# Row products, softmax inside PV and a V-moving last head in a one-token attention block

## The chip, the cores and the metric

One core of one Trainium2 chip. The metric is the device time of one execution in microseconds (us); one execution is also profiled. A ratio below is the mean time of one kernel's runs over that of the other's of the same rounds, with a 95% interval; so it is not quite the ratio of the medians quoted beside it. The verdict calls two kernels the same when they lie within 2%.

The engines in the profile are PE (matmuls), PEld (its weight loads), DVE (vector), ACT (activation), POOL, and SP, whose queue issues the loads here. PSUM is where matmuls put their results. PV is the product of the softmax's weights with V; a *turn* is a small f32 matmul that makes columns of rows; the *cadence* is the time from one head to the next.

## The reference, cut to what matters

One token of an adaLN-conditioned block: a modulation vector, a layer norm, attention with 32 query heads over 8 key/value heads and 32768 cached positions, the output projection, and a small feed-forward part.

```python
mod = (silu(c) @ w_mod).reshape(1, 6, 1, 512)          # w_mod 3 MB
h = layernorm(x) * (1 + ca) + sa
q = h @ wq                                             # wq 4 MB; 32 heads of 128
scores = einsum('bhqd,bhkd->bhqk', q, k) * 128**-0.5   # K cache 64 MB
o = einsum('bhqk,bhkd->bhqd', softmax(scores), v)      # V cache 64 MB
x = x + ga * (o.reshape(1, 1, 4096) @ wo)              # wo 4 MB
h = layernorm(x) * (1 + cb) + sb
return x + gb * (relu(h @ w1) @ w2)                    # 1.75 MB each
```

For each byte of K and V there is very little arithmetic: every byte is loaded once and used for four query heads.

## The kernel before

All loads go through one queue into a ring of four slots, in a fixed order (`stream`). A load is issued when its slot is free, that is, when the matmuls or transposes that read the slot's old content are done. (Cuts are marked `# ...`.)

```python
ring = ctx.enter_context(tc.tile_pool(name="ring", bufs=4))
stream = [("wm",), ("wq",)] + [("k", 0, (2 * G, 2 * G + 1)) for G in range(NG)]
for g in range(LAST):
    for G in range(NG):
        stream += [(kind, gg, (2 * G, 2 * G + 1)) for kind, gg in (("k", g + 1), ("v", g))]
stream += [("v", LAST, (0, 1)), ("v", LAST, (2,)), ("wo", 0), ("wo", 1), ("v", LAST, (3,)), ("wo", 2)]
stream += [("w1",)] + [("w2", i) for i in range(len(W2P))]
```

Modulation and queries are column products: the weights are the stationary operand, and each matmul gives one column of 128 values.

```python
for hq in range(Hq):
    for kt in range(KT):
        nc.tensor.matmul(qT_ps[:, hq:hq + 1], lhsT=wq_sb[:, kt, hq * Dh:(hq + 1) * Dh],
                         rhs=hT[:, kt:kt + 1], start=(kt == 0), stop=(kt == KT - 1))
```

For each head, DVE transposes K, PE forms the scores (S), the softmax follows, and PV multiplies with V. Heads 0 to 6 move V through PE (16x512 outputs). The last head has V stationary (columns), because its result is then there at once.

```python
def softmax(g):
    # ... row maximum m_p
    nc.tensor.transpose(out=mT_ps[:], in_=m_p[:], identity=ident_f[:])
    # ... maximum of each query head: Mrow, Mexp
    nc.tensor.matmul(Mb_ps[:], lhsT=Mexp[:], rhs=ident_f[0:1, 0:1], start=True, stop=True)
    # ... exponentials on ACT, P_g transposed on DVE to PT_g, Lexp
    nc.tensor.matmul(L_ps[:], lhsT=ones_f[:], rhs=Lexp[:], start=True, stop=True)

for g in range(Hkv):
    # ... build_qbd(g + 1)
    for G in range(NG):
        for u in (2 * G, 2 * G + 1):
            if g + 1 < Hkv:
                scores(g + 1, u)
        for u in (2 * G, 2 * G + 1):
            if g == LAST and u == NTILE - 1:
                for i in range(len(WOP) - 1):
                    project(i)          # first two parts of wo, as columns
            pv(g, u)
    if g + 1 < Hkv:
        softmax(g + 1)                  # after PV of head g
    normalise(g)
    # ...
project(len(WOP) - 1)                   # last part of wo, then the feed-forward part
```

## Time and profile before

| | before |
|---|---|
| median of 4 runs (the three of the prediction and one more) | 357.52 us (357.09 to 357.79) |
| profiled span, mean PE clock | 355.8 us, 0.876 |
| instructions; PE busy; DVE busy | 4200; 274.2 us; 188.0 us |
| loads | 149.43 MB; DMA share 1.00 from 20 to 340 us |

PE's timeline after PV of one head, before (columns: start, length, engine, line, operation, in brackets the idle time before and what ended it):

```profile
92.96 0.38 PE L371 MATMUL Mb_ps<-ident_f,Mexp 1*128 1x1 f32 x2
93.70 1.05 PE L429 MATMUL oT_ps<-osel,X 16*128 16x4 f32 x8 [0.36 <-ACT nbias L373]
96.59 0.45 PE L386 MATMUL L_ps<-Lexp,ones_f 128*128 128x4 f32 x2 [1.84 <-DVE Lexp L384]
99.50 1.87 PE L343 MATMUL S_ps<-KTt,qbd 128*128 128x512 bf16 x4 [2.47 <-DVE KTt L334]
```

From 92.96 to 99.50 PE does 1.9 us of small work and no score or PV matmul. The groups of the page that add this up over all heads (line, engine, operation, tiles, count, then busy us and mean ns, then idle time just before and its main releaser):

```profile
L343 PE MATMUL S_ps<-KTt,qbd 128*128 128x512 bf16 x512 | 134.5, 423 | 29.8 <-DVE KTt L334 29.7
L334 DVE STREAM_TRANSPOSE KTt<-Ksb 128x2048 f32<-128x2048 f32 x64 | 142.6, 2279 | 21.1 <-DMA Ksb<-in_A_k_cache_dram 17.0
L386 PE MATMUL L_ps<-Lexp,ones_f 128*128 128x4 f32 x16 | 3.9, 314 | 13.0 <-DVE Lexp L384 13.0
L359 PE MATMUL mT_ps<-ident_f,m_p 128*1 128x128 f32 x8 | 2.2, 269 | 8.4 <-DVE m_p L357 8.4
```

PE waits 13.0 us for the softmax sum and 8.4 for the maximum.

### The profile page before, as it was taken

What the parts mean: (1) busy time and instruction counts of PE and PEld (TensorE: products, weight loads), DVE (VectorE), ACT (ScalarE), POOL (GpSimd) and SP (SyncE); (2) the same over time, 40 slices, a digit from 0 to 9 for tenths busy, and PEclk for the clock granted to TensorE, in tenths of its full rate; (3) what the DMA queues carried; (4) which work ended last, traced back from release to release, by engine and by line L of the source; (5) the groups of instructions that cost most, each with busy time, mean ns of one, the idle gap of its engine ahead of it and who ended that gap; (6) DMA issues with size and microseconds to landing.
All of it is one profiled execution on the core that took longest, in us unless ns stands there. A gap on an engine that the chain in (4) does not pass through costs nothing.

```text
span 355.8 us, 4200 instructions
## 1 busy us (share of the span) xinstructions
PE 274.2 (77%) x1859; PEld 129.9 (37%) x1859; DVE 188.0 (53%) x210; ACT 30.8 (9%) x74; POOL 8.5 (2%) x14
## 2 busy tenths in 40 slices
PE   0552875998689885998499849987799859987754
PEld 0540322343333342443244324433243324335753
DVE  8414696783297409661759157642937184832020
ACT  1022002201200120001100120012000110003000
POOL 9000000000000000000000000000000000000000
PEclk9999968799969996999699978998599969997555
DMA  8999999999999999999999999999999999999993
GB/s 321 442 422 440 431 427 442 429 425 438 435 426 438 431 422 446 427 431 440 424 442 435 422 443 427 431 437 427 431 437 428 427 438 433 424 437 424 408 411 130
DMA packets 6604, 149.69 MB, mean 421 GB/s; under 512 B 697, under 2 KB 698, under 8 KB 1594
## 3 DMA queue, kind: packets, MB, share of 16 engines
q1 hardware_dynamic: 6578, 149.43, 97.9%
q8 instruction: 14, 0.23, 0.2%
q14 instruction: 4, 0.03, 0.0%
q10 hardware_dynamic: 8, 0.00, 0.0%
HBM read 149.42 MB, written 0.00 MB: 420 GB/s over the span
## 4 chain that ended last, share of the span: by engine, by line
DMA 47%; PE 34%; DVE 14%; issue 3%; ACT 0%; SPq 0%; DVEq 0%
DMA Ksb<-in_A_k_cache_dram 42%; PE S_ps L343 18%; PE o_ps L412 12%; DVE KTt L334 11%; DMA Vsb<-in_A_v_cache_dram 3%; DMA w_sb<-in_B_w_dram 2%; PE oT_ps L402 1%; DVE PT_g L381 1%; PE oT_ps L429 1%; DVE S_g L349 1%; PE L_ps L386 0%; SPq L118 0%; PE attnT_ps L461 0%; PE mT_ps L359 0%; ACT X L426 0%
## 5 line engine op out<-in xcount | busy, mean ns | idle before, releaser
L343 PE MATMUL S_ps<-KTt,qbd 128*128 128x512 bf16 x512 | 134.5, 423 | 29.8 <-DVE KTt L334 29.7
L334 DVE STREAM_TRANSPOSE KTt<-Ksb 128x2048 f32<-128x2048 f32 x64 | 142.6, 2279 | 21.1 <-DMA Ksb<-in_A_k_cache_dram 17.0
L412 PE MATMUL o_ps<-Vsb,PT_g 128*16 128x512 bf16 x448 | 99.0, 379 | 0.0
L343 PEld LDWEIGHTS <-qbd 128*128 128x128 bf16 x512 | 53.8, 106 | 104.6 <-issue 53.8
L412 PEld LDWEIGHTS <-PT_g 128*16 128x16 bf16 x448 | 39.1, 90 | 56.8 <-issue 3.0
L436 DVE TENSOR_TENSOR oT_sb<-oT_ps,Linv 128x4 bf16<-128x4 f32 x8 | 1.3, 162 | 71.8 <-PE oT_ps L429 57.3
L349 DVE TENSOR_SCALAR_CACHE_REDUCE S_g<-S_ps 128x512 f32<-128x512 f32 x16 | 11.1, 691 | 41.3 <-PE S_ps L343 41.3
L314 ACT COPY qbd<-qrep_sb 32x128 bf16<-32x128 bf16 x32 | 9.4, 295 | 160.0 <-PE S_ps L343 158.9
L386 PE MATMUL L_ps<-Lexp,ones_f 128*128 128x4 f32 x16 | 3.9, 314 | 13.0 <-DVE Lexp L384 13.0
L426 ACT COPY X<-o_ps 16x512 f32<-16x512 f32 x7 | 4.0, 574 | 110.4 <-PE o_ps L412 110.4
L402 PE MATMUL oT_ps<-PT_g,Vsb 128*128 128x4 bf16 x256 | 7.3, 166 | 4.4 <-DMA Vsb<-in_A_v_cache_dram 2.8
L381 DVE STREAM_TRANSPOSE PT_g<-P_g 128x1024 bf16<-128x1024 bf16 x8 | 9.9, 1232 | 0.0
L429 PE MATMUL oT_ps<-osel,X 16*128 16x4 f32 x56 | 7.3, 250 | 2.5 <-ACT nbias L373 2.5
L197 PE MATMUL xc_ps<-one,c_bd 8*128 8x1 bf16 x4 | 0.3, 172 | 11.6 <-DVE c_bd L187 11.6
L376 ACT ACTIVATE P_g<-S_g,nbias 128x1024 bf16<-128x1024 f32 x8 | 9.2, 1147 | 0.2
L402 PEld LDWEIGHTS <-Vsb 128*128 128x128 bf16 x256 | 7.2, 105 | 4.5 <-DMA Vsb<-in_A_v_cache_dram 2.9
L359 PE MATMUL mT_ps<-ident_f,m_p 128*1 128x128 f32 x8 | 2.2, 269 | 8.4 <-DVE m_p L357 8.4
L386 PEld LDWEIGHTS L_ps<-Lexp,ones_f 128*128 128x128 f32 x16 | 3.6, 271 | 13.5 <-issue 13.4
L155 DVE COPY sel<-ident_bf 128x128 bf16<-128x128 bf16 x4 | 7.8, 3823 | 0.4 <-POOL ident_bf masks.py:199 0.4
L429 PEld LDWEIGHTS oT_ps<-osel,X 16*128 16x128 f32 x56 | 6.7, 186 | 3.1 <-ACT nbias L373 3.1
L292 PE MATMUL qT_ps<-hT,wq_sb 128*128 128x1 bf16 x128 | 3.6, 165 | 3.2 <-DMA wq_sb<-in_A_wq_dram 3.2
L359 PEld LDWEIGHTS mT_ps<-ident_f,m_p 128*1 128x1 f32 x8 | 0.6, 80 | 12.2 <-issue 9.2
(94 smaller groups left out, 79.4 us busy)
## 6 DMA issues: line engine op xcount, KB each, us to landing
Ksb<-in_A_k_cache_dram SPq DMA_DIRECT2D x16, 4096.0 KB, 29.7
Vsb<-in_A_v_cache_dram SPq DMA_DIRECT2D x15, 4096.0 KB, 25.5
wq_sb<-in_A_wq_dram SPq DMA_DIRECT2D x1, 4096.0 KB, 19.7
Vsb<-in_A_v_cache_dram SPq DMA_DIRECT2D x2, 2048.0 KB, 15.5
wm_sb<-in_w_mod_dram SPq DMA_DIRECT2D x1, 3072.0 KB, 10.2
wo_sb<-in_A_wo_dram SPq DMA_DIRECT2D x1, 2048.0 KB
wo_sb<-in_A_wo_dram SPq DMA_DIRECT2D x2, 1024.0 KB, 10.2
w_sb<-in_B_w_dram SPq DMA_DIRECT2D x1, 1792.0 KB, 10.5
```

The lines of the kernel that those rows point to most:

```text
L155: nc.vector.tensor_copy(out=sel[:, hp, :].rearrange("p (a c) -> p a c", a=4), in_=src)
L314: nc.scalar.copy(out=o, in_=i)
L334: nc.vector.transpose(out=KTt[:].bitcast(F32), in_=Ksb[:, 32 * half:32 * half + 32, :].rearrange("p j d -> p (j d)").bitcast(F32),)
L343: nc.tensor.matmul(S_ps[:], lhsT=qbd[g % 2][:, hp, s, :], rhs=KTv[:, 16 * sl:16 * sl + 16, h, :, par], start=(t4 == 0 and sl == 0 and hp = ...
L349: nc.vector.tensor_scalar(out=S_tiles[g][:, G, :], in0=S_ps[:], scalar1=1.0, scalar2=None, op0=ALU.mult, op1=ALU.max, accum_out=m_tiles[g] ...
L376: nc.scalar.activation(out=P_g[:], in_=S_g[:].rearrange("p g f -> p (g f)"), func=ACT.Exp, bias=nbias[:], scale=scale, accum_out=l_g[:],)
L381: nc.vector.transpose(out=PT_g[:], in_=P_g[:])
L386: nc.tensor.matmul(L_ps[:], lhsT=ones_f[:], rhs=Lexp[:], start=True, stop=True)
L402: nc.tensor.matmul(o_tiles[g][:], lhsT=Vsb[:, j, :], rhs=PT_g[:, c0:c0 + REP], start=(u == 0 and j == 0), stop=(u == NTILE - 1 and j == TK ...
L412: nc.tensor.matmul(o_tiles[g][:], lhsT=PT_g[:, c0:c0 + 16], rhs=Vsb.rearrange("p (s j) d -> p s j d", j=16)[:, :, j, :], start=(u == 0 and ...
L426: nc.scalar.copy(out=X[:], in_=oT_ps[:])
L429: nc.tensor.matmul(oT_ps[:], lhsT=X[:, s * Dh:(s + 1) * Dh], rhs=osel[:, s, :], start=(s == 0), stop=(s == 3),)
```

## The change

The intent: fewer and larger instructions on PE, and no hole in PE's work at the end of each head.

- Modulation, queries and the first two parts of wo become row products: the vector is the stationary operand (one column), the weights move, and four one-row outputs sit at partitions 0, 32, 64 and 96. Small f32 matmuls turn the rows into columns again.
- The softmax is a generator, and its steps are placed between chunks of PV of the head before. PE gets a fixed order: 8 PV, maximum transpose, 8 PV, maximum broadcast, 16 PV, sum.
- The last head's first half of PV moves V, as in the other heads; only its second half stays in columns.
- A third PSUM bank for scores, and one shared PSUM accumulator. The order of the loads is unchanged.

```diff
-    ps_s = ctx.enter_context(tc.tile_pool(name="ps_s", bufs=2, ...))
+    ps_s = ctx.enter_context(tc.tile_pool(name="ps_s", bufs=3, ...))
 # ... one of the two new helpers for rows:
+    def to_rows(dst, src_T, w, n):
+        for kt in range(KT):
+            for j in range(n):
+                nc.tensor.matmul(
+                    dst[j // 4][32 * (j % 4):32 * (j % 4) + 1, :], lhsT=src_T[:, kt:kt + 1],
+                    rhs=w[:, kt, j * 512:(j + 1) * 512], start=(kt == 0), stop=(kt == KT - 1), ...)
 # ... queries (modulation likewise):
+    to_rows(q_ps, hT, wq_sb, 8)
+    nc.scalar.copy(out=q_rows[:, 0, :], in_=q_ps[0])
+    nc.vector.tensor_copy(out=q_rows[:, 1, :], in_=q_ps[1])
+    for i in range(2):
+        for m in range(4):
+            nc.tensor.matmul(qT_ps[:, i, m, :], lhsT=q_rows[:, i, m * Dh:(m + 1) * Dh], rhs=rowsel[:], ...)
 # ... softmax(g) gets two yields: after Mexp and after Lexp
 # ... last head, V stationary only in its second half:
-        if g == LAST:
+        if g == LAST and u > 1:
 # ... order of the heads:
+            if g + 1 < Hkv and G == NG - 1:
+                stages = softmax(g + 1)
+                pv(g, 2 * G, range(8))
+                next(stages)
+                pv(g, 2 * G, range(8, 16))
+                next(stages)
+                pv(g, 2 * G + 1)
+                next(stages, None)
+                continue
 # ... last head, before its last V quarter: project(i) now as rows, then
+                    join_rows()
-        if g + 1 < Hkv:
-            softmax(g + 1)
```

More of the change, by code (lines that the diff above doesn't have):

```diff
@@ L76 @@
     spool = ctx.enter_context(tc.tile_pool(name="spool", bufs=2))
-    ps_s = ctx.enter_context(tc.tile_pool(name="ps_s", bufs=2, space=bass.MemoryType.PSUM))
+    ps_s = ctx.enter_context(tc.tile_pool(name="ps_s", bufs=3, space=bass.MemoryType.PSUM))
     ps_o = ctx.enter_context(tc.tile_pool(name="ps_o", bufs=2, space=bass.MemoryType.PSUM))
@@ L181 @@
     oA = [const.tile([P, n * REP, P // (n * REP)], BF16, name=f"oA{i}") for i, (_, n) in enumerate(WOP)]
+    rowsel = const.tile([P, 4], F32)
+    nc.vector.tensor_copy(out=rowsel[:], in_=ident_f[:].rearrange("p (j c) -> p j c", c=32)[:, :, 0])
+    rowsum = const.tile([P, 1], F32)
+    nc.vector.reduce_sum(out=rowsum[:], in_=rowsel[:], axis=AX.X)
     one8 = const.tile([8, 1], BF16)
@@ L200, with bank, row_bank @@
     cT, xT = xc[:, 0, :], xc[:, 1, :]
-    attnT_ps = ps_acc.tile([P, KT], F32)
-    nc.vector.memset(attnT_ps[:], 0.0)
+    acc_ps = ps_acc.tile([P, REP + KT], F32)
+    nc.vector.memset(acc_ps[:], 0.0)
+    oT_ps, attnT_ps = acc_ps[:, 0:REP], acc_ps[:, REP:REP + KT]
+    def bank(name):
+        return ps_s.tile([P, 512], F32, tag="s", name=name)[:]
+    def row_bank(name):
+        t = bank(name)
+        nc.vector.memset(t, 0.0)
+        return t
     def layernorm_T(src_T, stat_in, dst_T, shiftT, nscaleT, tagp):
@@ L243, with rows_sb @@
     nc.vector.tensor_tensor(out=siluT[:], in0=cT, in1=sig[:], op=ALU.mult)
-    modT_ps = small_ps([P, NMOD], "modT_ps")
-    for j in range(6):
-        for ko in range(KT):
-            for kt in range(KT):
-                lhsT = wm_sb[:, kt, j * D:(j + 1) * D].rearrange("p (m ko) -> p ko m", ko=KT)
-                nc.tensor.matmul(
-                    modT_ps[:, j * KT + ko:j * KT + ko + 1], lhsT=lhsT[:, ko, :], rhs=siluT[:, kt:kt + 1],
-                    start=(kt == 0), stop=(kt == KT - 1),
-                )
-    modT_sb = const.tile([P, NMOD], F32)
-    nc.vector.tensor_copy(out=modT_sb[:], in_=modT_ps[:])
+    def to_rows(dst, src_T, w, n):
[3 more added lines that the diff above has]
+                    dst[j // 4][32 * (j % 4):32 * (j % 4) + 1, :], lhsT=src_T[:, kt:kt + 1],
+                    rhs=w[:, kt, j * 512:(j + 1) * 512], start=(kt == 0), stop=(kt == KT - 1),
+                    skip_group_check=True,
+                )
+    mod_ps = [row_bank(f"mod_ps{i}") for i in range(2)]
+    to_rows(mod_ps, siluT, wm_sb, 6)
+    def rows_sb(name):
+        return spool.tile([P, 2, 512], F32, tag="S_g", name=name)
+    mod_rows = rows_sb("mod_rows")
+    nc.scalar.copy(out=mod_rows[:, 0, :], in_=mod_ps[0])
+    nc.vector.tensor_copy(out=mod_rows[:, 1, :], in_=mod_ps[1])
+    modT_ps = small_ps([P, 2, KT, 4], "modT_ps")
+    for i in range(2):
+        for ko in range(KT):
+            nc.tensor.matmul(
+                modT_ps[:, i, ko, :], lhsT=mod_rows[:, i, :].rearrange("q (m ko) -> q ko m", ko=KT)[:, ko, :],
+                rhs=rowsel[:], start=True, stop=True,
+            )
+    modT_sb = const.tile([P, 8 * KT], F32)
+    nc.vector.tensor_copy(
+        out=modT_sb[:].rearrange("p (i j ko) -> p i ko j", i=2, j=4), in_=modT_ps[:],
+    )
     def rows4(src_T, r_ps, name):
@@ L269, in rows4 @@
         return r_sb
-    gb_ps = ps_s.tile([P, 512], F32, tag="s", name="gb_ps")[:, 0:P]
+    gb_ps = bank("gb_ps")[:, 0:P]
     nc.vector.memset(gb_ps, 0.0)
@@ L288 @@
     wq_sb = need(("wq",))
-    qT_ps = small_ps([P, Hq], "qT_ps")
-    for hq in range(Hq):
-        for kt in range(KT):
+    q_ps = [row_bank(f"q_ps{i}") for i in range(2)]
+    to_rows(q_ps, hT, wq_sb, 8)
+    q_rows = rows_sb("q_rows")
+    nc.scalar.copy(out=q_rows[:, 0, :], in_=q_ps[0])
+    nc.vector.tensor_copy(out=q_rows[:, 1, :], in_=q_ps[1])
+    qT_ps = small_ps([P, 2, 4, 4], "qT_ps")
+    for i in range(2):
+        for m in range(4):
             nc.tensor.matmul(
-                qT_ps[:, hq:hq + 1], lhsT=wq_sb[:, kt, hq * Dh:(hq + 1) * Dh],
-                rhs=hT[:, kt:kt + 1], start=(kt == 0), stop=(kt == KT - 1),
+                qT_ps[:, i, m, :], lhsT=q_rows[:, i, m * Dh:(m + 1) * Dh], rhs=rowsel[:], start=True, stop=True,
             )
     qT_sb = const.tile([P, Hq], BF16)
-    nc.scalar.copy(out=qT_sb[:], in_=qT_ps[:])
+    nc.scalar.copy(out=qT_sb[:].rearrange("p (i j m) -> p i m j", i=2, j=4), in_=qT_ps[:])
     qrep_ps = small_ps([P, 4, Hq], "qrep_ps")
@@ L328, in scores @@
         if u % 2 == 0:
-            S_ps_tiles[g] = ps_s.tile([P, 512], F32, tag="s", name="S_ps")
+            S_ps_tiles[g] = bank("S_ps")
         S_ps = S_ps_tiles[g]
@@ L343, in scores @@
                     nc.tensor.matmul(
-                        S_ps[:], lhsT=qbd[g % 2][:, hp, s, :], rhs=KTv[:, 16 * sl:16 * sl + 16, h, :, par],
+                        S_ps, lhsT=qbd[g % 2][:, hp, s, :], rhs=KTv[:, 16 * sl:16 * sl + 16, h, :, par],
                         start=(t4 == 0 and sl == 0 and hp == 0), stop=(t4 == 3 and sl == 1 and hp == 3),
@@ L349, in scores, with pe_order @@
                 nc.vector.tensor_scalar(
-                    out=S_tiles[g][:, G, :], in0=S_ps[:], scalar1=1.0, scalar2=None,
+                    out=S_tiles[g][:, G, :], in0=S_ps, scalar1=1.0, scalar2=None,
                     op0=ALU.mult, op1=ALU.max, accum_out=m_tiles[g][:, G:G + 1],
                 )
+    def pe_order(instr):
+        tc.stamp_issue_order_token(instr.ins, "pe_pv")
     def softmax(g):
@@ L358, in softmax @@
         mT_ps = small_ps([1, P], "mT_ps")
-        nc.tensor.transpose(out=mT_ps[:], in_=m_p[:], identity=ident_f[:])
+        pe_order(nc.tensor.transpose(out=mT_ps[:], in_=m_p[:], identity=ident_f[:]))
         Mrow = spool.tile([1, 4], F32, tag="Mrow", name="Mrow")
@@ L369, in softmax @@
         )
+        yield
         Mb_ps = small_ps([P, 1], "Mb_ps")
-        nc.tensor.matmul(Mb_ps[:], lhsT=Mexp[:], rhs=ident_f[0:1, 0:1], start=True, stop=True)
+        pe_order(nc.tensor.matmul(Mb_ps[:], lhsT=Mexp[:], rhs=ident_f[0:1, 0:1], start=True, stop=True))
         nbias = spool.tile([P, 1], F32, tag="nbias", name="nbias")
@@ L384, in softmax @@
         nc.vector.tensor_scalar(out=Lexp[:], in0=mask4, scalar1=l_g[:], scalar2=None, op0=ALU.mult)
+        yield
         L_ps = small_ps([P, REP], "L_ps")
@@ L389, in softmax, with pv @@
         Linv_tiles[g] = Linv
-    def pv(g, u):
-        PT_g = PT_tiles[g]
+    def pv(g, u, js=range(16)):
+        PT_g = PT_tiles[g][:].rearrange("p (h j c) -> p h j c", h=2, c=32)[:, u // 2]
+        s0 = 4 * (u % 2)
         Vsb = need(("v", g, u))
-        G, s0 = u // 2, 4 * (u % 2)
-        if g == LAST:
-            if u == 0:
-                o_tiles[g] = ps_o.tile([P, REP], F32, tag="oT", name="oT_ps", bufs=1)
+        if g == LAST and u > 1:
             for j in range(TK):
-                c0 = (16 * G + j % 16) * 32 + REP * (s0 + j // 16)
+                c0 = REP * (s0 + j // 16)
                 nc.tensor.matmul(
-                    o_tiles[g][:], lhsT=Vsb[:, j, :], rhs=PT_g[:, c0:c0 + REP],
-                    start=(u == 0 and j == 0), stop=(u == NTILE - 1 and j == TK - 1),
+                    oT_ps, lhsT=Vsb[:, j, :], rhs=PT_g[:, j % 16, c0:c0 + REP],
+                    start=False, stop=(u == NTILE - 1 and j == TK - 1), skip_group_check=True,
                 )
             return
-        if u == 0:
+        if u == 0 and js[0] == 0:
             o_tiles[g] = ps_o.tile([16, 4 * Dh], F32, tag="o", name="o_ps")
-        for j in range(16):
-            c0 = (16 * G + j) * 32 + REP * s0
-            nc.tensor.matmul(
-                o_tiles[g][:], lhsT=PT_g[:, c0:c0 + 16],
+        end = NTILE - 1 if g < LAST else 1
+        for j in js:
+            m = nc.tensor.matmul(
+                o_tiles[g][:], lhsT=PT_g[:, j, REP * s0:REP * (s0 + 4)],
                 rhs=Vsb.rearrange("p (s j) d -> p s j d", j=16)[:, :, j, :],
-                start=(u == 0 and j == 0), stop=(u == NTILE - 1 and j == 15),
+                start=(u == 0 and j == 0), stop=(u == end and j == 15),
             )
+            pe_order(m)
+        if u == end and j == 15:
+            X = spool.tile([16, 4 * Dh], F32, tag="X", name="X", bufs=1)
+            nc.scalar.copy(out=X[:], in_=o_tiles.pop(g)[:])
+            for s in range(4):
+                nc.tensor.matmul(
+                    oT_ps, lhsT=X[:, s * Dh:(s + 1) * Dh], rhs=osel[:, s, :],
+                    start=(s == 0), stop=(g < LAST and s == 3), skip_group_check=True,
+                )
     def part_of(g):
@@ L421, in normalise @@
     def normalise(g):
-        oT_ps = o_tiles.pop(g)
-        if g != LAST:
-            X = spool.tile([16, 4 * Dh], F32, tag="X", name="X")
-            nc.scalar.copy(out=X[:], in_=oT_ps[:])
-            oT_ps = ps_o.tile([P, REP], F32, tag="oT", name="oT_ps", bufs=1)
-            for s in range(4):
-                nc.tensor.matmul(
-                    oT_ps[:], lhsT=X[:, s * Dh:(s + 1) * Dh], rhs=osel[:, s, :], start=(s == 0), stop=(s == 3),
-                )
         i = part_of(g)
@@ L435, in normalise @@
         o_g = oT_sb[:, REP * g:REP * (g + 1)]
-        nc.vector.tensor_tensor(out=o_g, in0=oT_ps[:], in1=Linv_tiles.pop(g)[:], op=ALU.mult)
+        nc.vector.tensor_tensor(out=o_g, in0=oT_ps, in1=Linv_tiles.pop(g)[:], op=ALU.mult)
         nc.vector.tensor_tensor(
@@ L458, in project @@
         wo_sb = need(("wo", i))
+        if i < len(WOP) - 1:
+            if i == 0:
+                a_rows.append(row_bank("a_ps"))
+            for r in range(n):
+                nc.tensor.matmul(
+                    a_rows[0][32 * (r % 4):32 * (r % 4) + 1, :], lhsT=o2_tiles[i][:, r:r + 1],
+                    rhs=wo_sb[:, r, :], start=False, stop=(i == len(WOP) - 2 and r >= n - 4),
+                    skip_group_check=True,
+                )
+            return
         for r in range(n):
@@ L463, in project, with join_rows @@
                     lhsT=wo_sb[:, r, :].rearrange("p (m ko) -> p ko m", ko=KT)[:, ko, :],
-                    rhs=o2_tiles[i][:, r:r + 1], start=False, stop=(i == len(WOP) - 1 and r == n - 1),
-                    skip_group_check=True,
-                )
+                    rhs=o2_tiles[i][:, r:r + 1], start=False, stop=(r == n - 1), skip_group_check=True,
+                )
+    a_rows = []
+    def join_rows():
+        a_sb = rows_sb("a_sb")[:, 0, :]
+        nc.scalar.copy(out=a_sb, in_=a_rows[0])
+        for ko in range(KT):
+            nc.tensor.matmul(
+                attnT_ps[:, ko:ko + 1], lhsT=a_sb.rearrange("q (m ko) -> q ko m", ko=KT)[:, ko, :],
+                rhs=rowsum[:], start=False, stop=False, skip_group_check=True,
+            )
     build_qbd(0)
@@ L470 @@
         scores(0, u)
-    softmax(0)
+    for _ in softmax(0):
+        pass
     for g in range(Hkv):
@@ L490 @@
     project(len(WOP) - 1)
-    ffn_ps = ps_s.tile([P, 512], F32, tag="s", name="ffn_ps")[:, 0:P]
+    ffn_ps = bank("ffn_ps")[:, 0:P]
     nc.vector.memset(ffn_ps, 0.0)
-    x1_ps = ps_s.tile([P, 512], F32, tag="s", name="x1_ps")[:, 0:P]
+    x1_ps = bank("x1_ps")[:, 0:P]
     nc.vector.memset(x1_ps, 0.0)
@@ L498 @@
     x1T = const.tile([P, KT], F32)
-    nc.vector.tensor_tensor(out=x1T[:], in0=attnT_ps[:], in1=modT_sb[:, 2 * KT:3 * KT], op=ALU.mult)
+    nc.vector.tensor_tensor(out=x1T[:], in0=attnT_ps, in1=modT_sb[:, 2 * KT:3 * KT], op=ALU.mult)
     nc.vector.scalar_tensor_tensor(
```

## The prediction

> **What bounds the kernel now.** I read the page's slices first, because they say whether one resource is full in every stage, then the same in unequal stretches, then the queue that issues the loads, then the last microseconds. Slices of the span (busy tenths, granted TensorE clock, DMA, rate), and the load queue's total:
>
> ```profile
> PE   0552875998689885998499849987799859987754
> PEclk9999968799969996999699978998599969997555
> DMA  8999999999999999999999999999999999999993
> GB/s 321 442 422 440 431 427 442 429 425 438 435 426 438 431 422 446 427 431 440 424 442 435 422 443 427 431 437 427 431 437 428 427 438 433 424 437 424 408 411 130
> q1 hardware_dynamic: 6578, 149.43, 97.9%
> ```
>
> The reader should see that the PE row has holes and the clock row has dips, and that the DMA row has neither: only the first and last slices are below 9. The 149.43 MB of weights and cache are the kernel. Busy time by stretch (start:end, length; busy us of PE, its weight loads, DVE, ACT, POOL; clock; DMA share; GB/s):
>
> ```profile
> core 0: us, PE busy (x) PEld busy (x) DVE busy (x) ACT busy (x) POOL busy (x), PEclk, DMA share, GB/s
> 0.00:10.00 10.00, 0.00 (x0) 0.00 (x0) 8.79 (x10) 1.28 (x1) 8.48 (x14) 1.00 0.88 341
> 20.00:340.00 320.00, 260.21 (x1478) 117.15 (x1478) 173.17 (x165) 27.28 (x68) 0.00 (x0) 0.89 1.00 431
> 340.00:350.00 10.00, 7.02 (x207) 6.66 (x211) 2.02 (x14) 0.74 (x3) 0.00 (x0) 0.50 0.96 388
> ```
>
> For 320 us the DMA share is 1.00 at 431 GB/s. What is left outside the full stream, out of a span of 355.8 us: 1.8 us before the first packet (my reading of the packet records), 0.4 us of missing share in 340 to 350, and 4.3 us after the last packet at 351.5. So no change to PE, DVE or ACT work can gain more than about 5 us (1.4%), and only by touching the two ends.
>
> A full DMA row can still hide a kernel that is about to starve it, so I computed the reserve: bytes issued so far minus bytes moved so far (packet records), over 431 GB/s, at each issue. It is 23 to 24 us in the front (issues at 16.5 and 25.3), falls to 10.4 us at the issue at 68.24, stays between 11 and 19 us through the heads, and is smallest at the end: 7.7 us at 323.27, 2.4 us at 330.82, 4.3 at 334.23, 4.6 at 336.36, 4.8 at 344.27. The issues there, from the queue's timeline:
>
> ```profile
> 330.82 0.33 SPq L118 DMA_DIRECT2D Vsb<-in_A_v_cache_dram  x1
> 334.23 0.33 SPq L118 DMA_DIRECT2D wo_sb<-in_A_wo_dram  x1
> 336.36 8.25 SPq L118 DMA_DIRECT2D w_sb<-in_B_w_dram  x4
> ```
>
> Each waits for one of the four ring slots: the first for PV of the last head's V half, the second for its third quarter, the next for the wo products. Those are exactly the parts that the change rewrites, so 2.4 us is the number that decides. The end itself is a wait for data:
>
> ```profile
> 349.56 1.02 PE L525 MATMUL ffn_ps<-w_sb,hidT 128*1 128x128 bf16 x32 [0.98 <-DMA w_sb<-in_B_w_dram]
> 351.94 0.38 PE L525 MATMUL ffn_ps<-w_sb,hidT 128*1 128x128 bf16 x8 [0.50 <-DMA w_sb<-in_B_w_dram]
> 352.38 0.29 DVE L531 TENSOR_TENSOR o_rows<-ffn_ps,gb_rows_sb 128x128 f32<-128x128 f32 x1 [5.65 <-PE ffn_ps L525]
> 353.10 1.10 ACTq L534 DMA_DIRECT2D out_dram<-o_bf  x1
> ```
>
> All three pieces of w2 are waited for; only the 3.8 us after the last one is compute and output, and the change doesn't edit that code.
>
> **What the Trainium skill says.** "DMA: Bandwidth & Descriptors", section "Where 436 GB/s comes from": 16 SBUF ports at 435 GB/s cap one core. The trace's 431 GB/s agrees, so the rate has no room. "SBUF — State Buffer", section "Who interferes with whom": loads from the SP queue do not contend with compute engines; the trace agrees as far as the rate stays 415 to 459 GB/s in every 5 us window from 10 to 320 us, whether PE is busy 0.5 or 5 us of it. "TensorE: Matmul & The Clock Gate", "Part 3: Packing small matmuls — row/col tiling": products whose outputs sit at partitions 0, 32, 64, 96 run together. The trace agrees: in the fence above 32 products of 128 columns, written to four such rows at clock 0.50, take 1.02 us, 32 ns each, while 512-column matmuls at that clock come every 0.43 us, which is 107 ns for 128. Same page, "What's actually happening": the clock halves after a window of about 3.4 us without enough work. In this trace it is at 0.5 for 6.8 to 10.2 us after each head's softmax and from 325.4 to the end.
>
> **The change part by part.** The order of loads on the SP queue is identical in both programs, so only the times at which slots come free can move.
>
> Front, modulation: 96 column products took 3.33 us. Now 24 row products of 512 columns; column groups 0 and 1 get 8 each, so about 8 x 0.43 = 3.4 us cold. Added: a copy of 128x512 out of PSUM (an eviction of that size takes 0.69) and 8 f32 products with 128x128 weights. The L_ps matmuls have that shape and show 16 records for 8 calls at 314 ns, so 0.5 to 0.6 us a call, 4 to 5 us in all. Queries: 128 column products took 3.57 us; 32 row products are again 8 per group, 3.4 us, plus another copy and 8 turns, 5 us. With two PSUM memsets ahead of the first and two in between (some 1.5 us of DVE), first scores go from 33.79 to an estimated 39 to 42 us. Reserve: the wm slot comes free about 1 to 2 us later, against 23 us; the wq slot at 31 to 32 instead of 25.27, against 24; the first K slot some 6 us later than 40.34, against 18.9. None reaches zero. The delay is also partly paid back: scores of the second K half ran at clock 0.5 here (10.07 us for 32), after a gap; started later, with K already landed, they run back to back at 219 ns.
>
> Heads 0 to 6: softmax steps inside PV. Now, after PV ends at 92.96, PE does 2 us of small work until 99.50 while ACT exponentiates (1.15), DVE transposes P (1.24) and Lexp, L_ps follow. The new PE order is 8 PV, the max transpose, 8 PV, the max broadcast, 16 PV, then the sum: the chain of some 5 us lies beside 7.0 us of PV (32 x 219 ns). PE gains up to 4 us a head and loses fewer clock windows. K slots come free earlier, so the reserve grows. Worth in time: zero, for the DMA share is already 1.00.
>
> Third S bank, shared accumulator: no transfer depends on them; zero.
>
> Last head: the softmax is done before PV of head 6 ends. PV of head 6 can start at 315.0 instead of 316.16 and ends near 322.3; the X copy and turn take 1.8 us, so PV of the last head starts at 324.1 instead of 327.2. Its first half is now 32 moves of V at 219 ns, 7.0 us, instead of 128 column products in 3.4 us: done at 331.1 against 330.82. The 3 us saved by the softmax are eaten by the slower form: reserve 2.4 becomes 2.1 us. Then X and its turn (1.8 us) and 64 column products (1.8): 334.7 against 334.23. Row products of wo: 24, six per column group, 1.3 us warm or 2.6 cold, against 3.34: slots free at 336 to 337.3 against 336.36 and 337.43. Joining the rows (a copy and four f32 products, 2 to 3 us) ends by 340.3, when the last V quarter lands (PE resumed at 340.22 here). From there the same instructions in the same order.
>
> Sum: front 0, heads 0, last head 0 to +0.5, tail -0.1 (if the clock stays up, the last 8 products take 0.2 less). I predict 357.3 us, no change from 357.33.
>
> **Rivals.** *The reserve breaks at the end.* For: 2.4 us is small; an issue takes 1.0 us to its first packet at the start (0.74 to 1.76); the window from 322 to 325.4 is half idle in the new order too, and if the clock halves there, PV's first half ends near 332.8, reserve 0.4, and about 0.6 us is lost; a second dip at the row products could make it 1 to 2. Against: the engines drain unevenly (DMA busy decays from 349 to 351.5), so the slowest, which sets the end, has more queued than the mean. Time: 358 to 359. *The front starves the queue*, because the f32 turns cost more than their model or row products don't run together (then 10 and 14 us cold): scores would start at 55 to 60, the 10.4 us at 68.24 would be spent, and up to 5 us lost: 360 to 362. Against: L525 shows the groups running together. *PE and DVE were the limit*, as the chain of waits suggests with PE 34% and DVE 14%: seven heads x 4 us would give 330. Against: that share is only the route by which the chain goes back through the ring; bytes over rate alone give 347 us.
>
> **Range and chances.** Three runs before spread 0.7 us. The upside is the tail and the 0.4 us of missing share; the downside is the two starvation rivals. Range 356.6 to 358.6. Beyond 2% faster (350.2) lies below what the stream takes with its ends; beyond 2% slower (364.5) needs 7 us of idle DMA. Chances: 1% faster, 97% within 2%, 2% slower.
>
> **What would show it.** Right: DMA share 1.00 and about 431 GB/s from 20 to 340 with last packet near 351.5; first scores near 40 us without a DMA dip; PE idle after each head's PV gone, the clock row higher, the waits on Lexp gone, and the queue issuing earlier in the heads; the V load of 330.82 issued at 331 to 333. Wrong: a DMA share under 0.95 at 60 to 100 or 330 to 345, or a different rate at a full share, which I have no mechanism for.

## The result, and the profile after

| | before | after |
|---|---|---|
| median of 4 runs | 357.52 us (357.09 to 357.79) | 357.38 us (357.00 to 357.88) |
| ratio after/before, 95% | | 0.9998 (0.9979 to 1.0018) |
| profiled span, mean PE clock | 355.8 us, 0.876 | 356.0 us, 0.887 |
| instructions; PE busy; DVE busy | 4200; 274.2; 188.0 us | 3635; 287.1; 191.6 us |
| last load packet ends | 351.5 us | 351.76 us |

The time is the same. 565 instructions fewer, and no hole inside the softmax any more, changed nothing that can be measured. The slices of the span, after:

```profile
PE   0466965999699969788896969896978879799874
PEclk9966789999879998999899969999899969899755
DMA  8999999999999999999999999999999999999993
```

The DMA row is as full as it was. The stretches (columns as in the prediction's table: PE, PEld, DVE, ACT, POOL, clock, DMA share, GB/s):

```profile
20.00:340.00 320.00, 271.49 (x1284) 116.55 (x1284) 176.27 (x175) 31.14 (x72) 0.00 (x0) 0.90 1.00 430
330.00:340.00 10.00, 8.59 (x111) 5.34 (x109) 0.00 (x0) 2.44 (x3) 0.00 (x0) 0.69 0.97 391
340.00:350.00 10.00, 7.00 (x190) 6.56 (x191) 2.03 (x14) 0.74 (x3) 0.00 (x0) 0.50 1.00 399
```

Share 1.00 again from 20 to 340, with a dent of 0.3 us in 330 to 340 where the kernel before had none, and none in 340 to 350 where that one lost 0.4. PE's timeline in the same head as above, now with the softmax steps inside PV:

```profile
83.82 1.89 PE L458 MATMUL o_ps<-Vsb,PT_g 128*16 128x512 bf16 x8
85.65 0.27 PE L404 MATMUL mT_ps<-ident_f,m_p 128*1 128x128 f32 x1
85.85 1.89 PE L458 MATMUL o_ps<-Vsb,PT_g 128*16 128x512 bf16 x8
87.67 0.38 PE L417 MATMUL Mb_ps<-ident_f,Mexp 1*128 1x1 f32 x2
87.98 3.62 PE L458 MATMUL o_ps<-Vsb,PT_g 128*16 128x512 bf16 x16
91.53 0.39 PE L433 MATMUL L_ps<-Lexp,ones_f 128*128 128x4 f32 x2
92.26 1.05 PE L468 MATMUL acc_ps<-osel,X 16*128 16x4 f32 x8 [0.35 <-ACT X L466]
96.01 1.44 PE L384 MATMUL S_ps<-KTt,qbd 128*128 128x512 bf16 x3 [2.70 <-DVE KTt L375]
```

From the first PV to the sum there are no brackets, so no waits: the edit does there what it was written for. The hole is not closed to the end: after the sum PE still waits 2.70 us for K's transpose before it can form the next scores (2.47 us before). Where did the saved time go? The page's groups that answer to those of before:

```profile
L384 PE MATMUL S_ps<-KTt,qbd 128*128 128x512 bf16 x512 | 135.6, 423 | 39.1 <-DVE KTt L375 39.1
L375 DVE STREAM_TRANSPOSE KTt<-Ksb 128x2048 f32<-128x2048 f32 x64 | 142.5, 2280 | 34.4 <-DMA Ksb<-in_A_k_cache_dram 32.8
```

PE's wait for the sum is gone from the view of the waits, and that for the maximum is down from 8.4 to 1.1 us. But PE now waits 39.1 us instead of 29.7 for K's transpose, and DVE waits 32.8 us instead of 17.0 for K's bytes. The saving has become waiting for data: 15.8 us more of it on DVE.

The load queue at the end of the span, after; each start answers to one in the prediction's fence (330.82, 334.23, 336.36):

```profile
331.68 0.33 SPq L118 DMA_DIRECT2D Vsb<-in_A_v_cache_dram  x1
335.22 0.33 SPq L118 DMA_DIRECT2D wo_sb<-in_A_wo_dram  x1
337.04 1.24 SPq L118 DMA_DIRECT2D w_sb<-in_B_w_dram  x2
```

Each is issued 0.7 to 1.0 us later than before. The reserve at the first (bytes issued minus bytes moved, over 431 GB/s) is 1.4 us instead of 2.4. In this stretch packets of unchanged size take longer: their excess over the usual duration sums to 8.7 us of engine time in 320 to 340 (4.7 before), half a microsecond for each of 16 engines. The last waits:

```profile
351.50 1.02 PE L601 MATMUL ffn_ps<-w_sb,hidT 128*1 128x128 bf16 x24 [0.26 <-DMA w_sb<-in_B_w_dram]
352.57 0.29 DVE L607 TENSOR_TENSOR o_rows<-ffn_ps,gb_rows_sb 128x128 f32<-128x128 f32 x1 [5.65 <-PE ffn_ps L601]
```

The end is still a wait for the last weights, and the last DVE work starts at 352.57 instead of 352.38.

### The profile page after: what moved, and what is told of

Read it like the earlier page. It is cut to its first block, busy times and chain, and to the rows that moved or that the text cites. A ratio compares the mean times of both kernels' runs of the same rounds, so it can differ in the third digit from the quotient of the medians.

```text
span 356.0 us, 3635 instructions
## 1 busy us (share of the span) xinstructions
PE 287.1 (81%) x1571; PEld 128.5 (36%) x1571; DVE 191.6 (54%) x219; ACT 34.0 (10%) x78; POOL 8.5 (2%) x14
## 4 chain that ended last, share of the span: by engine, by line
DMA 55%; PE 22%; DVE 16%; issue 4%; ACT 1%; SPq 0%; DVEq 0%; ACTq 0%
DMA Ksb<-in_A_k_cache_dram 50%; DVE KTt L375 14%; PE S_ps L384 9%; PE o_ps L458 6%; DMA c_row<-in_c_dram 3%; DMA w_sb<-in_B_w_dram 2%; PE modT_ps L284 1%; PE acc_ps L448 1%; PE q_ps L267 1%; PE mod_ps L267 1%; PE a_ps L510 1%; PE qT_ps L334 1%; PE acc_ps L468 1%; PE acc_ps L530 1%; ACT L243 0%
## 5 line engine op out<-in xcount | busy, mean ns | idle before, releaser
L384 PE MATMUL S_ps<-KTt,qbd 128*128 128x512 bf16 x512 | 135.6, 423 | 39.1 <-DVE KTt L375 39.1
L375 DVE STREAM_TRANSPOSE KTt<-Ksb 128x2048 f32<-128x2048 f32 x64 | 142.5, 2280 | 34.4 <-DMA Ksb<-in_A_k_cache_dram 32.8
L458 PE MATMUL o_ps<-Vsb,PT_g 128*16 128x512 bf16 x480 | 108.4, 379 | 0.0
L458 PEld LDWEIGHTS <-PT_g 128*16 128x16 bf16 x480 | 40.8, 90 | 60.0 <-issue 6.0
L468 PE MATMUL acc_ps<-osel,X 16*128 16x4 f32 x64 | 8.4, 250 | 3.2 <-ACT X L466 3.2
L419 ACT ACTIVATE nbias<-Mb_ps 128x1 f32<-128x1 f32 x8 | 1.4, 171 | 89.1 <-PE Mb_ps L417 89.1
L468 PEld LDWEIGHTS acc_ps<-osel,X 16*128 16x128 f32 x64 | 7.7, 186 | 4.3 <-ACT X L466 4.3
L406 DVE TENSOR_REDUCE Mrow<-mT_ps 1x4 f32<-1x128 f32 x8 | 2.2, 278 | 8.2 <-PE mT_ps L404 8.2
L267 PE MATMUL q_ps<-wq_sb,hT 128*1 128x512 bf16 x32 | 3.6, 627 | 2.6 <-DVE hT L250 2.6
L435 DVE RECIPROCAL Linv<-L_ps 128x4 f32<-128x4 f32 x8 | 1.4, 176 | 7.0 <-PE L_ps L433 7.0
L417 PEld LDWEIGHTS Mb_ps<-ident_f,Mexp 1*128 1x128 f32 x16 | 2.3, 182 | 6.1 <-issue 6.1
L284 PE MATMUL modT_ps<-rowsel,mod_rows 128*128 128x4 f32 x16 | 3.9, 375 | 0.5 <-ACT mod_rows L279 0.5
## 6 DMA issues: line engine op xcount, KB each, us to landing
Ksb<-in_A_k_cache_dram SPq DMA_DIRECT2D x16, 4096.0 KB, 29.7
wm_sb<-in_w_mod_dram SPq DMA_DIRECT2D x1, 3072.0 KB, 10.3
```

The source lines that it names most:

```text
L267: nc.tensor.matmul(dst[j // 4][32 * (j % 4):32 * (j % 4) + 1, :], lhsT=src_T[:, kt:kt + 1], rhs=w[:, kt, j * 512:(j + 1) * 512], start=(kt ...
L284: nc.tensor.matmul(modT_ps[:, i, ko, :], lhsT=mod_rows[:, i, :].rearrange("q (m ko) -> q ko m", ko=KT)[:, ko, :], rhs=rowsel[:], start=Tru ...
L375: nc.vector.transpose(out=KTt[:].bitcast(F32), in_=Ksb[:, 32 * half:32 * half + 32, :].rearrange("p j d -> p (j d)").bitcast(F32),)
L384: nc.tensor.matmul(S_ps, lhsT=qbd[g % 2][:, hp, s, :], rhs=KTv[:, 16 * sl:16 * sl + 16, h, :, par], start=(t4 == 0 and sl == 0 and hp == 0 ...
L458: m = nc.tensor.matmul(o_tiles[g][:], lhsT=PT_g[:, j, REP * s0:REP * (s0 + 4)], rhs=Vsb.rearrange("p (s j) d -> p s j d", j=16)[:, :, j, : ...
L468: nc.tensor.matmul(oT_ps, lhsT=X[:, s * Dh:(s + 1) * Dh], rhs=osel[:, s, :], start=(s == 0), stop=(g < LAST and s == 3), skip_group_check= ...
```

## The experiments

My theory: the stream of loads sets the time in both kernels; the change makes room for compute in the heads, which nothing uses; the end of the stream, with its small reserve, is the only place where compute can still cost time. The rivals: something else than the stream sets the 357 us (then more compute in the heads would cost time, and taking compute away would gain a lot), or gain and loss of two parts of the change cancel. The experiments build on the changed kernel unless said otherwise. They were in four groups, each with its own runs of the kernel before on the same chip, and the ratios are to those.

### Loads alone

All loads in the same order, no compute except a copy of the last w2 to the output. The result is wrong.

```diff
-    # ... all compute
+    while pos[0] < len(stream):
+        load(stream[pos[0]])
+        pos[0] += 1
+    w2_last = loaded[("w2", len(W2P) - 1)]
+    nc.vector.tensor_copy(out=o_bf[:], in_=w2_last[:, 0, 0, 0:P])
```

> The changed kernel's loads, in the same order through the same four ring slots, with all compute removed; the output is a copy of the last w2 piece, so it is wrong on purpose. Theory (the load stream sets the time, compute is hidden): the last packet still ends near 351.5 us, only the last products and the two output steps go, about 0.9 us; 356.0 to 357.0 us. Rival (compute costs time through late slots, and gains and losses of the change cancelled): well below that, towards bytes over rate plus the ends, 353 us or less.

Measured: 353.87 us (353.74 to 354.04), ratio 0.9902 (0.9887 to 0.9917). The expectation missed by 2 us, in a telling way. First, removing all compute gains only 3.5 us, so the stream does set the time, up to these 3.5 us. Second, the DMA share was just as full in both kernels, and still the last packet ends at 349.08 instead of 351.76. Something in the real kernels takes 2.7 us of a DMA row that looks full; another 1.0 us is the shorter tail. This asked for the next two runs.

### Loads with PE busy, and loads with many small PE instructions

The loads-only kernel plus independent matmuls: 1571 of 512 columns (as many PE instructions as the changed kernel has), or twice as many of 4 columns.

```diff
+    for i in range(1571):
+        nc.tensor.matmul(j_ps[i % 2][:], lhsT=jw[:], rhs=jx[:], start=True, stop=True)
 # second kernel:
+    for i in range(3142):
+        nc.tensor.matmul(j_ps[i % 2][:, 0:4], lhsT=jw[:], rhs=jx[:, 0:4], start=True, stop=True)
```

> The loads alone again, plus 1571 matmuls (the changed kernel's number) on constant tiles that no load waits for; about 344 us of PE work at 219 ns, output wrong on purpose. The stream alone took 353.87 us, 2.7 us earlier at its last packet than the changed kernel. Theory A (instruction fetch: the 12 packets of 16 KB, 0.9 us each, that the changed kernel's trace shows on the same DMA engines, put single engines behind): they return here, the last packet moves from 349.1 to 350 to 351 and the time to 354.8 to 356. Theory B (late slots near the end of the real kernel alone cost the 2.7 us): 353.9, within 0.3.

> The loads alone plus 3142 matmuls of 4 columns: twice the instructions of the run with 1571 matmuls of 512 columns, but little PE work. The loads alone took 353.87, with 1571 large matmuls 356.07. Theory A (instruction fetch on the DMA engines): about 24 fetch packets in place of 12, so about twice the 2.2 us, 357.5 to 359. Theory B (the PE's work or its reads of SBUF slow the loads): less than 354.5.

Measured: 356.07 us (355.84 to 356.30), ratio 0.9972 (0.9955 to 0.9989), with the last packet at 350.90; and 357.81 us (357.62 to 358.01), ratio 1.0017 (1.0002 to 1.0032), last packet at 352.55. The queue lines of the two pages, first the large matmuls, then the small ones:

```profile
q8 instruction: 12, 0.20, 0.2%
```

```profile
q8 instruction: 24, 0.39, 0.4%
```

The kernel of loads alone has no packet of this kind. So 0, 12 and 24 fetches of instructions go with 353.87, 356.07 and 357.81 us (three groups of runs, in which the kernel before took 357.42, 357.29 and 357.26). PE is busy for 341.6 us in the first of these two and 87.1 in the second, which is the slower one; so it is not PE's work or its reading of SBUF that costs the stream time. What grows with the cost is the number of PE's instructions, and the fetch packets are what the trace shows of them on the DMA engines. The times agree: in the second run the last fetch comes at 158.2; the issues of loads are 3.6 us behind those of the loads alone at 121.5 (121.50 against 117.89), and still 3.5 at the last one (344.13 against 340.63). That it is the fetch, and nothing else that goes with an instruction, is the likely reading; no run separates the two. Each fetch packet of 16 KB took 0.88 to 0.99 us where a data packet of that size took 0.61. Twelve of them are 11 us of engine time, 0.7 us if spread over 16 engines; the runs with them take 2.2 longer. That they fall on a part of the engines, so that these finish last, would explain it. The trace does not name the engine of a packet, but the drain fits: from 3.5 to 1.5 us before the last packet ends, the DMA share is still full with the loads alone (345.6 to 347.6), 0.68 with 12 fetches (347.4 to 349.4) and 0.53 with 24 (349 to 351), so that in the last case about half of the engines are done early. Which ones the fetches fall on stays open.

The kernel before has 14 such packets and the changed one 12. By this measure (my estimate: 2 packets at 3.94 us for 24) the shorter program should be 0.3 us faster; that is too little for these runs to show.

### More PV in the heads

In heads 0 to 6, 16 more PV matmuls at the start of PV, overwritten by the real ones; the result stays right. Per head 16 x 0.219 = 3.5 us of PE.

```diff
+        extra = 1 if (g < LAST and u == 0) else 0
+        for k in range(16 * extra):
+            nc_m = nc.tensor.matmul(o_tiles[g][:], lhsT=PT_g[:, k % 16, REP * s0:REP * (s0 + 4)],
+                rhs=Vsb.rearrange("p (s j) d -> p s j d", j=16)[:, :, k % 16, :], ...)
+            pe_order(nc_m)
```

> The changed kernel with 16 more PV matmuls (a pass that is thrown away) in each of heads 0 to 6: 7 x 16 x 219 ns = 24.5 us more PE work, result unchanged. Theory (hidden behind the loads, reserve of 10 to 19 us): 357.4 us, within 0.7; the reserve at the issues in the heads falls by some us but not to zero. Rival (PE or the PE-DVE chain sets the time): up to 382 us.

Measured: 362.64 us (362.36 to 362.93), ratio 1.0144 (1.0128 to 1.0161). Missed: I had expected all of it to be hidden. Within the heads it is: the DMA share is 1.00 from 40 to 320. The lag comes out at the end (stretch 320 to 340):

```profile
320.00:340.00 20.00, 18.93 (x129) 9.20 (x127) 3.44 (x11) 2.56 (x5) 0.00 (x0) 1.00 0.73 295
```

The V load that the changed kernel issues at 331.68 is issued at 337.35 with nothing left in the queue, and DMA idles for some 5 us. The issues of V in successive heads are 39.2 us apart (156.88 to 313.88 in four heads). The loads of one head are 16.78 MB, at 433 GB/s 38.75 us. So the compute of a head takes about 39.2 - 3.5 = 35.7 us in the changed kernel: it has room for some 3.0 us a head, and 3.5 was too much. The excess of 0.45 us over seven heads is 3.2 us; the V load came 5.7 us later. The rest shows in the reserve: the changed kernel works off the lag that the front leaves (reserve 10.5 us at 67.93, 19.1 at 156.50), while with 16 extra matmuls it stays low (11.4 at 66.96, 9.0 at 156.88, 7.4 at 313.88). The lesson for the theory: there is room, but it is 3 us a head and not unlimited.

### Less extra, in both kernels

Half as much, 8 more PV matmuls (1.75 us) a head, in the changed kernel and in the kernel before. This is the experiment that tells whether the placed softmax did anything.

```diff
-        for k in range(16 * extra):
+        for k in range(8 * extra):
```

> The changed kernel with 8 more PV matmuls (thrown away) in each of heads 0 to 6, 12.3 us in all. With 16 a head its cadence was 39.2 us (issues at 156.88 to 313.88), a little over the 38.75 us that a head's loads take, and the lag met the small reserve at the end. Theory (compute cadence 35.7 us a head, so 3 us of room; with 8 it is 37.5 and the lag is worked off): 357.4, within 0.6. Rival (any extra PE work costs a fixed part): half of the 5.2 us of the run with 16, 360.0.

> The same 8 matmuls a head in the kernel before. Its cadence while it caught up was 38.05 us a head (97.25 to 135.30 in the chain), so 39.8 with them, over the 38.75 of the loads: the initial lag is never worked off. Theory (the change bought room that the load stream hides): 362 to 367 us, where the changed kernel stays at 357.4. Rival (both kernels are equally far from being compute-bound): the same time as the changed kernel with 8, within 0.6.

Measured: 357.48 us (357.31 to 358.23), ratio 1.0014 (0.9999 to 1.0029), in the changed kernel; 366.27 us (364.94 to 366.68), ratio 1.0250 (1.0228 to 1.0271), in the kernel before. In the changed kernel 12.3 us of added PE work cost nothing that these runs resolve, and in the other the same work cost 9 us. The stretch from 40 to 340, first the changed kernel with the extra, then the kernel before with it:

```profile
40.00:340.00 300.00, 268.41 (x1241) 113.80 (x1239) 167.57 (x161) 26.12 (x59) 0.00 (x0) 0.93 1.00 431
```

```profile
40.00:340.00 300.00, 255.22 (x1192) 109.52 (x1191) 163.60 (x158) 24.19 (x57) 0.00 (x0) 0.91 0.98 421
```

The rate stays 431 in the one and falls to 421 in the other. The slices of the second show where:

```profile
DMA  8999999999999999999999999999999999995594
```

The row is full for 36 slices, so up to 330 us the page looks healthy. The reserve tells the story earlier: at the V issues it sinks head by head, 9.8, 7.9, 7.8, 6.7, 5.3, 3.2 us, and reaches 0 at 333.5. V issues are 39.97 us apart (77.53 to 277.40 in five heads; the last one included, 40.1), so the compute of a head before the change takes about 38.2 us: room 0.6 us against 3.0 after, each good to some 0.2 us. So the change is worth about 2.5 us a head, and 1.75 us of extra is 1.2 over the old room. The V load that the kernel before issues at 330.82 with 2.4 us queued goes out here at 341.09 with nothing queued: 10.3 us later, 7.9 beyond the reserve, of the 9.0 measured.

### The changed kernel with the old place of the softmax, and the same extra

This undoes only the placement, to attribute the room to it.

```diff
-            if g + 1 < Hkv and G == NG - 1:
+            if False:
 # ... after the PV of head g:
+        if g + 1 < Hkv:
+            for _ in softmax(g + 1):
+                pass
```

> The changed kernel with 8 more PV matmuls a head, and the softmax steps back after PV; row products, third S bank and the last head as in the change. With the steps inside PV this load cost nothing (357.48), in the kernel before it cost 366.27. Theory (the room comes from the placement of the softmax steps alone): 366 to 373, at or above the kernel before, because here the max transpose also comes after PV and the last head's slower form no longer has the softmax beside it. Rival (other parts of the change give room as well): below 362.

Measured: 375.12 us (373.82 to 376.26), ratio 1.0505 (1.0470 to 1.0541), 2 us above the expected range. The direction is as expected: without the placement the room is gone, so rows, third bank and accumulator alone do not give it. The V issues are 40.2 us apart (78.70 to 320.09 in six heads), against 40.1 over the same six in the kernel before with the extra (77.53 to 318.24). The last V load:

```profile
348.85 0.33 SPq L118 DMA_DIRECT2D Vsb<-in_A_v_cache_dram  x1
```

In the kernel before with the extra it is issued at 341.09. The 7.8 us between are in the two traces: the last head's sum (L_ps) comes at 339.06 against 337.09, 2.0 us later, and from PV's start to the issue its first half takes 9.3 us in the V-moving form (339.55 to 348.85, its first 11 matmuls 0.43 us apart, as at the granted clock of 0.5) against 3.6 in columns (337.51 to 341.09). So 5.8 of the 7.8 us are the last head's V-moving form, which here has no early softmax to make up for it. That also means that the 375.12 us are not the placement in the heads alone.

### More PV in the last head

32 more PV matmuls (7.0 us) in the last head only.

```diff
+        extra = 2 if (g == LAST and u == 0) else 0
+        for k in range(16 * extra):
+            # ... matmul as above
```

> The changed kernel with 32 more PV matmuls (thrown away) before the first V half of the last head: 7.0 us, less than a third of the extra work of the run before, but where the reserve is 1.4 us. Theory (reserve): the V load issued at 331.7 moves to 338.7 and the stream runs dry: 7.0 - 1.4 plus or minus 1 for the issue latency and for slower DMA engines that have more queued: 361.5 to 364.0 us. Rival (hidden as well): 357.4. Rival (the end is a compute chain): the full 7.0, 364.4.

Measured: 363.94 us (363.14 to 364.38), ratio 1.0181 (1.0166 to 1.0196), as expected. The stretch from 330 to 340:

```profile
330.00:340.00 10.00, 9.93 (x57) 4.48 (x56) 0.00 (x0) 0.57 (x1) 0.00 (x0) 1.00 0.40 147
```

DMA is busy for 0.40 of it: 6 us lost. The V load came at 338.31. Of 7.0 us added at this place 6.6 come through (363.94 less 357.38); 12.3 us, spread over the heads in the run with 8 extra, cost nothing. The reserve at each place says which is which: 1.4 us here, 9 to 19 there (8.6 at 79.93 the least).

### The last head's first half back in columns

```diff
-        if g == LAST and u > 1:
+        if g == LAST:
```

> The changed kernel with the last head's first V half back in the old form (128 column products in place of 32 moves of V). Theory: PV of that half takes 3.4 us instead of 7.0, the load at 331.7 goes out near 328.5 and the reserve there rises from 1.4 to about 4.5 us; the time stays 357.4 within 0.5, because the stream was not dry there. Rival (the last head's V move costs or saves time): a difference of 1 us or more.

Measured: 357.25 us (356.83 to 357.59), ratio 0.9996 (0.9981 to 1.0011). The V load:

```profile
327.93 0.33 SPq L118 DMA_DIRECT2D Vsb<-in_A_v_cache_dram  x1
```

It is issued 3.75 us earlier than in the changed kernel, with a reserve of 5.2 us instead of 1.4, and the excess time of packets in 320 to 340 falls from 8.7 to 1.3 us. So the V-moving form spends the head start that the placed softmax gives the last head (2.9 us, 327.93 against 330.82), and 0.9 us more. In time it makes no difference that these runs can resolve, since 1.4 us was still enough. It is the version that I would keep, for its reserve; it does not measurably beat either kernel.

### Without the V loads

To see the compute of both kernels without the stream: V is loaded once into its own buffer and used for all heads, the ring has three slots (kernel before, changed kernel, changed kernel with the old place of the softmax). Their outputs are wrong, which doesn't matter for the times. The comparison with the reference would not notice a wrong V.

```diff
-    ring = ctx.enter_context(tc.tile_pool(name="ring", bufs=4))
+    ring = ctx.enter_context(tc.tile_pool(name="ring", bufs=3))
+    v_one = vpool.tile([P, TK, Dh], BF16, name="v_one")
+    stream_dma(v_one[:], vv[0, :, 0:TK, :])
 # ... need(): every ("v", ...) returns v_one; no V in the stream
```

> The kernel before with V loaded once (one quarter of head 0, used for every head, result wrong on purpose) and three ring slots for the rest: 84 MB in place of 149, about 196 us of loads, so compute sets the time. Sum from the trace: softmax of head 1 done at 97.25, six more heads at 38.05, then 22 us to the end: 347 to 351 us.

> The same for the changed kernel. Theory (the change makes compute shorter by about 2.3 us a head, which the full kernel hides): 93.65, six heads at 35.7, then some 30 us: 337 to 342 us, 2 to 4% below the kernel before in the same form. Rival (the change is neutral in compute too, or its slower last head and front eat the gain): within 1% of the kernel before in this form.

> The changed kernel without V loads, with the softmax steps back after PV and everything else of the change kept. Theory (the placement is what shortens compute): back up to 346 to 352, at or a little above the kernel before in this form. Rival (row products or the third S bank do it): stays within 3 us of the changed kernel in this form.

Measured: 302.84 us (302.45 to 304.39), ratio 0.8486; 311.70 us (310.15 to 314.10), ratio 0.8732; 312.50 us (310.17 to 314.57), ratio 0.8768. All three expectations missed, and the order of before and after is the opposite of what I wrote. The reason is in the timelines: without V loads the instruction order that the build chooses is another. In the kernel before and in the one with the old place, 21 or 22 score matmuls of the next head stand between the broadcast of the maximum and the sum; in the changed kernel such matmuls stand between the chunks of PV and after the sum. So the hole is gone in all three, and the compute of a head is 29.9, 30.3 and 29.9 us. The runs therefore do not compare what they were meant to, and say nothing on the room in the real kernels. Two things remain of them. The 38.2 us of the kernel before are a matter of order, not of work. And from the last scores to the end the three take 35.6, 38.1 and 41.4 us: in this form, what follows the last scores is slower by 2.5 to 5.8 us in the changed kernels.

## Why the prediction was right

**The bound.** Right. The loads alone take 353.87 us, and 12.3 us of added PE work in the changed kernel costs nothing. One part was incomplete: I counted what is outside the full stream (start, dent, tail) as all that could be gained (the three terms add up to 6.5 us, of which I called about 5 the most; taking away all compute gained 3.5), and missed that instruction fetches lie inside the full share. The run with as many of them as the changed kernel has took 2.2 us more than the loads alone, which the miss of the loads-only run brought out. Together: 353.87 for the loads, 2.2 with twelve fetches, and 1.3 that are left over and fit the longer tail and the late, uneven end, make the 357.4. The section of the Trainium skill that the prediction cites for the rate ("DMA: Bandwidth & Descriptors", "Where 436 GB/s comes from") also states a limit of some 358 GB/s on the side of HBM, and that it binds for loads from HBM; the prediction leaves this out. The 431 GB/s measured on this one core are above it, so of the section's two limits it is the 435 that agrees.

**Front.** The row products took 3.33 and 3.58 us against 3.4, the modulation turns 3.90 against 4 to 5. The query turns took 2.14, not 5. First scores came at 34.89, not at 39 to 42; this step failed. PE's timeline, first before, then after:

```profile
25.52 0.27 PE L300 MATMUL qrep_ps<-qT_sb,sel 128*128 128x32 bf16 x4 [0.28 <-ACT qT_sb L297]
33.79 9.49 PE L343 MATMUL S_ps<-KTt,qbd 128*128 128x512 bf16 x32 [8.01 <-DVE KTt L334]
```

```profile
31.94 0.25 PE L341 MATMUL qrep_ps<-qT_sb,sel 128*128 128x32 bf16 x4 [0.32 <-ACT qT_sb L338]
34.89 9.67 PE L384 MATMUL S_ps<-KTt,qbd 128*128 128x512 bf16 x32 [2.69 <-DVE KTt L375]
```

The queries are ready 6.4 us later, much as the terms say. But the first scores had been waiting 8.01 us for K's transpose after that, and I added the delay to a start that queries did not set. The wait took up 5.3 us of it. Nor did the scores of the second K half run back to back: they took 8.48 us for 32, after a wait of 3.02 us as before (10.06 us before). The step had no effect on the total, as the reserve was 20.1 us at the first delayed issue and never under 10.5 in the front; so the right total does not vouch for it.

**Heads.** Right in sign and in worth: the waits on Lexp are gone, the room per head went from about 0.6 to 3.0 us, and the time did not move. "Up to 4 us a head" is about 2.5 as measured. "PE idle after each head's PV gone, the clock row higher" held at most by half: the hole inside the softmax is gone, but after the sum PE still waits for K's transpose (2.70 us in the head shown), and the mean clock of 0.887 against 0.876 is no rise: the four runs after have 0.882 to 0.905, the 28 runs of the kernel before in the four groups 0.880 to 0.899.

**Last head.** PV of the last head started at 324.57 (predicted 324.1), the V load was issued at 331.68 (331.1, with 331 to 333 allowed), wo's rows took 2.73 us (1.3 to 2.6), and the joined rows were done at 340.6 (340.3). The rival *the reserve breaks at the end* came within sight: the clock halved after about 333.7, the reserve fell to 1.4 us, and 0.3 us of DMA share was lost. It did not break. (The prediction calls all three late parts rewritten; the third quarter of V kept its form.) The 0.1 us forecast for the tail did not come: the clock stayed at 0.50 to the end, and the last DVE work started 0.2 us later.

**Third bank, shared accumulator.** Not tried alone. The total leaves no room for an effect worth telling.

**The expected gain** of the edit is thus located: it was made, off the path that sets the end, and it turned into waiting for data (DVE, 17.0 to 32.8 us). At the end of the stream it was spent on a slower form of the last head, as the run with columns shows.

## What to carry to other kernels

When the DMA row is full, compute the reserve, bytes issued minus bytes moved, at each issue. In this case added compute was free where it was some 9 us or more and the head had room, and where it was 1.4 us, 6.6 of 7.0 added microseconds came through. A change of compute in such a kernel buys room instead of time, and adding known work until the time moves measures that room (here 0.6 us a head before, 3.0 after). Count the instructions too: their fetch shares the DMA engines with the data, and here the loads took 2.2 us longer with 12 such packets and 3.9 with 24.

## What the Trainium skill lacked or had wrong

- "Runtime: NRT & Kernel Launch", section "Instruction fetch mechanics": the blocks of 16 KiB and 256 instructions agree with the runs (1571 matmuls with their weight loads: 12 fetches; 3142: 24). It calls the cost of a block "mostly hidden". In a program bound by loads this did not hold: it took 2.2 us longer with 12 fetches and 3.9 us longer with 24, from 353.87 us without any.
- "SBUF — State Buffer", section "Who interferes with whom": that compute does not hold up loads agrees as to PE's use of SBUF (341.6 us of busy PE cost less than 87.1 us with twice the instructions). It does not speak of instruction fetch, which loads the same DMA engines with 12 and 24 packets of 16 KB here.
- "TensorE: Matmul & The Clock Gate", "Part 3: Packing small matmuls — row/col tiling", has figures for three column tiles (2.38 times), none for four. Here 32 products of 512 columns onto one-row outputs at four partitions (in two banks) took 3.58 us, 112 ns each, with the granted clock at 0.50; 512-column products that are not packed come every 0.43 us at that clock: about 3.8 times.
- No page has the reserve as a measure: the DMA row of the page reads 9 alike with 1.4 and with 20 us of queued bytes, and 7.0 us of added work cost 6.6 us at the first place while 12.3 us cost nothing over the heads.
